# M of batch 1's third chunk, made after the states' reads instead of beside M of batch 0's last chunk

## The chip, the cores and the metric

The kernel runs on one core of one Trainium2 chip. The metric is the device time of one execution in microseconds (us), taken as the median of several runs. Four runs of the kernel before are given; they lie between 710.19 and 710.21 us, with a median of 710.2 us.

## What is computed

The reference is an attention block whose result is fed through a feed-forward block. Cut to what matters (B = 8 batches, H = 8 heads, S = 512 tokens, 32 states, D = 64 per head, so a row of 512 after the heads are joined, and d_ff = 2048):

```
a      = softmax(scale * x @ state.T)        # over the 32 states
xread  = a @ state                           # (B, H, 512, 64)
a2     = softmax(scale * state @ x.T)        # over the 512 tokens
sread  = a2 @ x                              # (B, H, 32, 64)
rows   = concatenate([xread, sread], axis=2) # heads joined: 4352 rows of 512
h      = rows @ w_in
g      = h * sigmoid(1.702 * h)
out    = g @ w_out
```

## The kernel before

**How the work is cut.** xread is never formed. Since xread @ w_in = a @ (state @ w_in), the kernel first makes, for a batch b and one of four chunks c of 512 columns of d_ff, the product M(b, c) of the states with that part of w_in (`att_M`, matmuls by `by_state`, line L320). Then `up_x` (through `up`, L524) multiplies M by the transposed softmax aT to get 128 rows of h for all 512 tokens, and ScalarE applies the activation (L527) into a buffer g. Four `up_x` steps use one chunk of M; sixteen make one batch's g. `down` (L542) multiplies g by w_out into four PSUM banks, one for each 128 tokens.

**What one M takes.** M(b, c) has two halves of 128 x 512 numbers, each filling one PSUM bank. Its sixteen matmuls use 64 rows and 32 columns of TensorE's array each. They are issued in two passes of eight, which run side by side. ScalarE then copies the two banks to the SBUF tile M (L460), and only after its copy is a bank free.

**Which banks.** Two banks are in the pool psA (tag `att`), and two in psH (tag `h`). `up_x` takes a bank of psH, or one of psA where it is called with `spare`. `att_M` takes both banks of psA, or both of psH with `spare` (its third argument True). The remaining four banks hold scores and then the results of `down`.

**Order.** Every engine works off its own list of instructions in the order in which the program writes them; the order is written out by hand. For batches 0 and 1 it is: a first part that loads, rounds the weights and makes scores; then `turn(b, c, then, n, more)`, which does the four `up_x` of chunk c of batch b and, ahead of the last of them, makes the M named in `then` (and in `more`); `rounds` brings in pieces of w_out, seven VectorE instructions for each (L207 to L243). The call that matters is the one for batch 0, chunk 2: ahead of its last `up_x` (h tile 11) it makes M(0, 3) in psA and M(1, 2) in psH.

After it, ScalarE does the four exponentials of the states' softmax (`att_s_exp`, L372), with a load of its table before and after; VectorE scales the results (`att_s_norm`, L378 to L381) and rounds more of w_out; TensorE does h tiles 12 to 15, which use M(0, 3). Then a loop over f (0 to 15) does the sixteen `down` steps of batch 0. Between them, at f = 0, stand four groups of transposes (`att_eT`, L489); at f = 1 the states' reads of batches 0 and 1 (`att_sread`, matmuls L500 into one bank of psA each, ScalarE's copy L506) and then M(1, 3) in psA; at f = 2 two small transposes (`att_srT`, L514) and the first `up_x` that reads M(1, 2), h tile 8 of batch 1; the other `up_x` of batch 1 follow at f = 3, 5, 7 and so on.

From batch 1's own `down` on, a fixed sequence of Strassen products follows (`strassen_two`, `strassen_low`, `up_strassen`; L738, L689, L1051), with the next batch's attention hung in at named points ("P2a", "P5.1", "run").

Of the kernel before, what the change touches and what calls it, by code (L numbers as in the profile page):

```python
# [20 lines left out]
def kernel(  # L21
# [70 lines left out]
    def att_ps(shape, name):  # L92
        return psA.tile(shape, FP32, tag="att", name=name)
# [36 lines left out]
    def load_state(b):  # L130
        stn[b] = apool.tile([P, NG, D], FP32, tag="stn", name=f"stn_{b}", bufs=2)
        for g in range(NG):
            nc.sync.dma_start(stn[b][:, g], st_v[b, g])
# [9 lines left out]
    def load_x_squares(b):  # L143
        xsq[b] = xpool.tile([P, NPR, S], FP32, tag="xn", name=f"xsq_{b}")
        for g in range(NG):
            for k in range(D // Ns):
                o = D * g + Ns * k
                dst = xsq[b][o : o + Ns].rearrange("p j (t a) -> p j t a", a=Ns)
                for j in range(NPR):
                    nc.sync.dma_start(dst[:, j], x_sq[b, g, k][:, j])  # L150

    def turn_x(b):

        A[b]["xT"] = xsq[b]
        for j in range(NPR):
            nc.vector.transpose(xsq[b][:, j], xsq[b][:, j])
# [106 lines left out]
    def round_to(n, ahead=AHEAD):  # L263

        nin = NFC * NPR
        while done["b"] < min(n, len(PIECES)):
            i = done["b"]
            powers_to(i + 1)
            round_b(i, min(i + 1 + ahead, max(nin, i + 1)), i + 1 < nin and (i + 1 < n or i >= NPR))
            done["b"] += 1  # L270
            while done["b"] > NPR and done["load"] < len(PIECES) and before(done["load"]) < done["b"]:
                load_weights(done["load"] + 1)
# [42 lines left out]
    def by_state(b, ps, rhs):  # L315

        for j in range(NPR):
            for g in range(NG):
                rows, st = slice(D * g, D * (g + 1)), slice(Ns * j, Ns * (j + 1))
                nc.tensor.matmul(ps[g][st], A[b]["stT"][rows, st], rhs(rows, j), start=True, stop=True)  # L320
# [32 lines left out]
    def att_s_max(b):  # L353
        a = A[b]
        a["mx2"] = []
        for g in range(NG):
            mx = apool.tile([P, 1], FP32, tag="mx2", name=f"mx2_{b}_{g}", bufs=4)
            nc.vector.tensor_reduce(out=mx, in_=a["s"][g], axis=AX.X, op=ALU.max, negate=True)
            nc.vector.tensor_scalar(mx, mx, scale, None, ALU.mult)
            a["mx2"].append(mx)  # L360
# [90 lines left out]
    def att_M(b, c, spare=False):  # L451

        m = mpool.tile([P, NG, FC], FP32, tag=f"M{turns['M'] % NFC if b < 2 else c}", name=f"M_{b}_{c}")
        turns["M"] += 1
        A[b]["M", c] = m
        name = f"M_{b}_{c}_"
        ps = [psH.tile([P, FC], FP32, tag="h", name=name + str(g)) if spare else att_ps([P, FC], name + str(g)) for g in range(NG)]
        by_state(b, ps, lambda rows, j: w_in[c][rows, j])
        for g in range(NG):
            nc.scalar.copy(m[:, g], ps[g])  # L460
# [21 lines left out]
    def att_eT(b, g):  # L482

        a = A[b]
        if g == 0:
            a["eT"] = apool.tile([P, NG, SCH, P], FP32, tag="e1" if b else "eT", name=f"eT_{b}")
        ps = att_ps([P, SCH, P], f"eT_{b}_{g}")
        for c in range(SCH):
            nc.tensor.transpose(ps[:, c], a["e2"][g][0][:, P * c : P * (c + 1)], ident)  # L489
        nc.scalar.copy(a["eT"][:, g], ps)  # L490

    def att_sread(b):

        a = A[b]
        ps = att_ps([P, NG, D], f"sr_{b}")
        for g in range(NG):
            for c in range(SCH):
                for j in range(NPR):
                    st = slice(Ns * j, Ns * (j + 1))
                    nc.tensor.matmul(  # L500
                        ps[st, g], a["eT"][:, g, c, st], xn[b][:, c, NG * j + g],
                        start=(c == 0), stop=(c == SCH - 1),
                    )
        sr = apool.tile([P, P], FP32, tag="sr", name=f"sr_{b}", bufs=2)
        if b < 2:
            nc.scalar.copy(sr, ps.rearrange("p g d -> p (g d)"))  # L506
        else:
            for g in range(NG):
                nc.scalar.activation(out=sr[:, D * g : D * (g + 1)], in_=ps[:, g], func=AF.Copy, scale=a["e2"][g][1])
        A[b]["sr"] = sr  # L510

    def att_srT(b):
        ps = att_ps([P, P], f"srT_{b}")
        nc.tensor.transpose(ps, A[b]["sr"], ident)  # L514
        nc.scalar.copy(srT[:, :, b, :], ps.rearrange("p (j n) -> p j n", j=NPR))
# [13 lines left out]
    def up_x(b, f, spare=False):  # L529
        c, o = divmod(P * f, FC)  # L530
        m = A[b]["M", c]
        up(b, f, S, [m[:, g, o : o + P] for g in range(NG)], [A[b]["aT"][:, g] for g in range(NG)], spare)
# [3 lines left out]
    def down(key, r, fs, dst, last):  # L536

        if fs[0] == 0:
            O[key, r] = bank_o[r]
        ops = O[key, r]  # L540
        for f in fs:
            nc.tensor.matmul(  # L542
                ops, G[key, f // 2][:, f % 2, P * r : P * (r + 1)], w_out[:, f], start=(f == 0), stop=(f == NF - 1)
            )
            if last and f < HF and f % 2:
                free.append(G.pop((key, f // 2)))
        if fs[-1] == NF - 1:
            osb = opool.tile([P, DM], FP32, tag="osb", name=f"osb_{key}_{r}")
            nc.scalar.copy(osb, ops)
            nc.sync.dma_start(dst, osb)  # L550
# [9 lines left out]
    def s12(key, u, ntok):  # L560

        half = ntok // 2
        (a11, a21), (_, a22) = quarters(key, u, ntok), quarters(key, HF // 2 + u, ntok)
        s1, s2 = S1[:, 2 * u : 2 * u + 2, :half], S2[:, 2 * u : 2 * u + 2, :half]
        nc.vector.tensor_tensor(out=s1, in0=a21, in1=a22, op=ALU.add)
        nc.vector.tensor_tensor(out=s2, in0=s1, in1=a11, op=ALU.subtract)
# [109 lines left out]
    def low_third(t):  # L676
        _, b12, _, b22 = halves_of(t)
        T_of(b12, b22, b12)
# [441 lines left out]
    def rounds(n):  # L1120
        round_to(done["b"] + n)
# [44 lines left out]
    round_to(NPR + 1)  # L1166
    att_x_norm(1)

    def turn(b, c, then, n=(), more=None):

        for i in range(nper):
            if i == nper - 1 and then:
                att_M(*then)
                if more:
                    att_M(*more)
            up_x(b, nper * c + i)
            if i < len(n):
                rounds(n[i])
# [6 lines left out]
    round_to(4 * NPR)  # L1185
    att_s_max(0)
    att_s_max(1)
    turn(0, 2, (0, 3), more=(1, 2, True))
    room = apool.tile([P, NPR, S], FP32, tag="xT", name="e2_01")
    att_s_exp(0, room[:, :NG])  # L1190
    att_s_exp(1, room[:, NG:])
# [12 lines left out]
    def T_of(t, x0, x1):  # L1204
        nc.vector.tensor_tensor(out=t, in0=x0, in1=x1, op=ALU.subtract)

    def low_made(k, t, i):

        for fn, args in low_sums(t, (low_a, low_b)[i]):
            fn(*args)  # L1210
        low_keep(k, turn_rooms[i])

    def low_away(k, t):

        room = apool.tile([P, NPR, S], FP32, tag="xT", name=f"away_{k}").rearrange("p j t -> p (j t)")[:, : 3 * FC]
        for fn, args in low_sums(t, low_parts(room)):
            fn(*args)
        low_keep(k, room)
# [3 lines left out]
    for f in range(NF):  # L1222
        rounds(1)
        round_to(NFC * NPR + f + 1)
        if f == NF - 1:

            up_x(1, rest.pop(0))
        for r in range(SCH):
            down(0, r, [f], out_x[0, r], r == SCH - 1)
        if f == 0:  # L1230
            for b in range(2):
                for g in range(NG):
                    att_eT(b, g)
        if f == 1:

            att_sread(0)
            att_sread(1)
            att_M(1, 3)
        if f == 2:
            att_srT(0)  # L1240
            att_srT(1)
        if f == 2 or f % 2 == 1 and 1 < f < NF - 1:
            up_x(1, rest.pop(0))
        if f == HF:
            load_state(2)
            load_x_squares(2)
        if f == NF - 2:
            T_of(T1, B12, B11)
            low_away(6, B22)
            low_made(5, T1, 1)  # L1250
            for u in range(NU - 1):
                s12(1, u, S)
            T_of(T2, B22, T1)
            low_third(T1)
            for u in range(NU - 1):
                s3(1, u, S)
            T_of(B12, B22, B12)
            low_away(3, T3)
            low_third(T3)
        if f == NF - 1:  # L1260
            turn_x(2)
            low_made(2, T2, 0)
# [73 lines left out]
```

## Time and profile before

| | |
|---|---|
| median of the runs | 710.2 us |
| the profiled execution's own time | 710.21 us |
| its span, first to last instruction | 708.4 us |
| TensorE (PE) busy | 695.9 us, 98% of the span |
| VectorE (DVE) busy | 601.9 us, 85% |
| ScalarE (ACT) busy | 231.3 us, 33% |
| DMA traffic | 77.89 MB, mean 110 GB/s |

The profiled execution took 1.8 us more than its span, which lies ahead of the first and after the last instruction. PE stands for matmuls, PEld for the loads of their weights (the stationary operand), which overlap matmuls. A tile's number is left out in the rows: all M tiles, PSUM banks of M included, are called M. An "idle before" names what ended the wait. Busy time of a pipelined matmul overlaps that of its neighbour, so for TensorE the distance from one start to the next is what counts.

### The profile page before, as it was taken

Reading aid. Unit: us, or ns where it says so; the run is one execution under the profiler, and the core shown is the slowest. Engines: PE = TensorE matmul, PEld = TensorE weight load, DVE = VectorE, ACT = ScalarE, POOL = GpSimd, SP = SyncE. Lnnn points to the kernel's source line nnn. Section 1 sums busy time; section 2 is a strip of 40 time slices with the busy share of each in tenths; the row PEclk is TensorE's granted clock in tenths of the full one; section 3 lists DMA queues with packets and bytes.
Section 4 is the critical chain, followed back from the end, with each engine's and each line's share of the span. In section 5 each row is a group of like instructions: output and inputs, shape, how many; then the busy total and the mean of one; then the engine's idle time right before and its main releaser. Section 6 shows DMA issues by size and latency. Waiting matters only on the chain.

```text
span 708.4 us, 12667 instructions
## 1 busy us (share of the span) xinstructions
PE 695.9 (98%) x4973; PEld 558.0 (79%) x4975; DVE 601.9 (85%) x1246; ACT 231.3 (33%) x456; POOL 0.8 (0%) x8
## 2 busy tenths in 40 slices
PE   8989999999999999999999999999999999999996
PEld 3433444458998799879998899889987998899995
DVE  6999699999978998799978996899789987888650
ACT  5686610014224412423233423341243224300210
POOL 0000000000000000000000000000000000000000
PEclk9999999999999999999999999999999999999999
DMA  9921246318742384409550664148432840041001
GB/s 234 366 71 57 82 149 146 126 75 206 217 118 44 61 194 136 79 1 206 153 107 1 142 189 119 20 80 197 137 53 45 193 152 16 0 121 60 16 1 29
DMA packets 143914, 77.89 MB, mean 110 GB/s; under 512 B 113904, under 2 KB 127728, under 8 KB 143856
## 3 DMA queue, kind: packets, MB, share of 16 engines
q1 hardware_dynamic: 143856, 77.09, 41.6%
q8 instruction: 39, 0.64, 0.4%
q14 instruction: 19, 0.16, 0.1%
HBM read 61.08 MB, written 15.99 MB: 109 GB/s over the span
## 4 chain that ended last, share of the span: by engine, by line
PE 96%; ACT 2%; DMA 1%; DVE 0%; issue 0%; DVEq 0%
PE low L689 21%; PE o L1051 17%; PE o L738 14%; PE o L689 10%; PE o L542 8%; PE h L524 7%; PE upx L1051 6%; PE M L320 4%; PE o L585 2%; PE warm L125 2%; PE o L320 1%; PE sr L500 1%; PE upx_sr L1051 1%; DMA out_dram<-osb_sr 1%; ACT M L460 1%; ACT low L219 1%
## 5 line engine op out<-in xcount | busy, mean ns | idle before, releaser
L1061 DVE TENSOR_TENSOR g<-o,g 128x512 f32<-128x512 f32 (+1 forms) x140 | 88.0, 650 | 51.1 <-PE o L1051 50.2
L738 PE MATMUL o<-w_out,g 128*128 128x256 f32 x448 | 100.5, 380 | 0.0
L738 PEld LDWEIGHTS o<-w_out,g 128*128 128x128 f32 x448 | 84.2, 190 | 16.9 <-issue 5.5
L1058 ACT ACTIVATE g<-g 128x512 f32<-128x512 f32 (+1 forms) x84 | 49.8, 600 | 100.8 <-DVE g L1061 100.8
L1051 PE MATMUL upx<-aT,M 128*128 128x256 f32 x192 | 49.3, 379 | 0.0
L1051 PE MATMUL o<-ta,M 128*128 128x256 f32 x192 | 49.3, 379 | 0.0
L1051 PE MATMUL o<-ta,ms 128*128 128x256 f32 x192 | 48.3, 379 | 0.0
L689 PE MATMUL low<-low,g 128*128 128x128 f32 x336 | 44.4, 275 | 0.0
L689 PEld LDWEIGHTS low<-low,g 128*128 128x128 f32 x336 | 40.9, 192 | 0.0
L460 ACT COPY M<-M 128x512 f32<-128x512 f32 x64 | 33.1, 597 | 23.3 <-PE M L320 23.3
L1051 PEld LDWEIGHTS o<-ta,ms 128*128 128x128 f32 x192 | 36.5, 190 | 5.0
L1051 PEld LDWEIGHTS o<-ta,M 128*128 128x128 f32 x192 | 36.5, 190 | 5.0
L1051 PEld LDWEIGHTS upx<-aT,M 128*128 128x128 f32 x192 | 36.0, 190 | 4.6
L689 PE MATMUL low<-sums,later 128*128 128x128 f32 x280 | 37.0, 275 | 0.0
L689 PEld LDWEIGHTS low<-sums,later 128*128 128x128 f32 x280 | 34.6, 192 | 0.4
L320 PE MATMUL M<-w_in,stT 64*32 64x512 f32 x512 | 32.4, 594 | 0.0
L527 ACT ACTIVATE g<-h 128x512 f32<-128x512 f32 x24 | 14.0, 592 | 54.7 <-PE h L524 54.7
L524 PE MATMUL h<-low,M 128*128 128x512 f32 x64 | 29.5, 597 | 1.5 <-DVE low L408 1.5
L524 PE MATMUL h<-aT,M 128*128 128x512 f32 x64 | 28.7, 599 | 2.3 <-ACT M L460 2.3
L689 PE MATMUL low<-w_out,g 128*128 128x128 f32 x224 | 29.6, 275 | 0.0
L542 PE MATMUL o<-w_out,g 128*128 128x512 f32 x64 | 28.6, 594 | 0.0
L542 PE MATMUL o<-w_out,sums 128*128 128x512 f32 x64 | 28.3, 592 | 0.0
(210 smaller groups left out, 1295.7 us busy)
## 6 DMA issues: line engine op xcount, KB each, us to landing
low<-low SPq DMA_DIRECT2D x78, 256.0 KB, 3.5
later<-in_moe_w_out_dram SPq DMA_DIRECT2D x16, 512.0 KB, 3.3
xn<-in_x_dram SPq DMA_DIRECT2D x28, 256.0 KB, 4.8
low<-low SPq DMA_DIRECT2D x9, 768.0 KB, 4.0
w_out<-in_moe_w_in_dram SPq DMA_DIRECT2D x12, 512.0 KB
xsq<-in_x_dram SPq DMA_DIRECT2D x96, 64.0 KB, 2.3
out_dram<-osb SPq DMA_DIRECT2D x18, 256.0 KB, 2.8
out_dram<-later SPq DMA_DIRECT2D x14, 256.0 KB, 2.2
```

Of the source, the lines that this page charges most:

```text
L125: nc.tensor.matmul(ps, zeros[:, :P], zeros, start=True, stop=True)
L320: nc.tensor.matmul(ps[g][st], A[b]["stT"][rows, st], rhs(rows, j), start=True, stop=True)
L460: nc.scalar.copy(m[:, g], ps[g])
L524: nc.tensor.matmul(hps, lhs[i], rhs[i], start=(i == 0), stop=(i == n - 1))
L527: nc.scalar.activation(out=G[key, f // 2][:, f % 2, :ntok], in_=hps, func=AF.Gelu_apprx_sigmoid)
L542: nc.tensor.matmul(ops, G[key, f // 2][:, f % 2, P * r : P * (r + 1)], w_out[:, f], start=(f == 0), stop=(f == NF - 1))
L585: nc.tensor.matmul(ps[:, r], lhs[f][:, P * r : P * (r + 1)], rhs[:, f], start=(first and r == 0 and f == 0), stop=(f == HF - 1), skip_grou ...
L689: nc.tensor.matmul(ps, lhs[f], rhs[:, f], start=(first and f == 0), stop=(f == QF - 1), skip_group_check=True)
L738: nc.tensor.matmul(ps[:, r], lhs[f][:, P * r : P * (r + 1)], rhs[:, f], start=(r == 0 and f == 0), stop=(f == HF - 1), skip_group_check=True,)
L1051: nc.tensor.matmul(ps[:, k], lhs[i][:, o : o + P], rhs[i], start=(first and k == 0 and i == 0), stop=(i == n - 1), skip_group_check=True,)
L1058: nc.scalar.activation(out=dst, in_=src, func=AF.Gelu_apprx_sigmoid)
L1061: nc.vector.tensor_tensor(out=dst, in0=ps, in1=x, op=ALU.add)
```

## The change

M(1, 2) is no longer made in the turn of batch 0's third chunk. It is made at f = 1 of the loop over `down`, after the two states' reads and ahead of M(1, 3). It still takes the two banks of psH, and M(1, 3) those of psA. The SBUF tile that it is copied to is given out in turn by a counter; since M(1, 2) still comes after M(0, 3) and ahead of M(1, 3), each M gets the same tile as before. The parameter `more` of `turn` goes.

```diff
-    def turn(b, c, then, n=(), more=None):
+    def turn(b, c, then, n=()):
 
         for i in range(nper):
             if i == nper - 1 and then:
                 att_M(*then)
-                if more:
-                    att_M(*more)
             up_x(b, nper * c + i)
             if i < len(n):
                 rounds(n[i])
...
     att_s_max(0)
     att_s_max(1)
-    turn(0, 2, (0, 3), more=(1, 2, True))
+    turn(0, 2, (0, 3))
     room = apool.tile([P, NPR, S], FP32, tag="xT", name="e2_01")
...
             att_sread(0)
             att_sread(1)
+            att_M(1, 2, True)
             att_M(1, 3)
         if f == 2:
```

Moved are, on TensorE, 16 weight loads and 16 matmuls of L320, and on ScalarE two copies of L460. VectorE, GpSimd and the DMA queue of SyncE keep their instructions and their order.

## The prediction

> **What bounds the kernel now.** I read the page's chain of work first: it says who ended last.
>
> ```profile
> PE 96%; ACT 2%; DMA 1%; DVE 0%; issue 0%; DVEq 0%
> ```
>
> TensorE is the bound almost everywhere, so a microsecond that TensorE does not wait, or does not work, counts in full unless something else then comes late. Next I read the places where the chain is not TensorE's. This is the same chain around the change (start, length, engine and line), in order of time:
>
> ```profile
> 68.25 1.16 PE M L320 x16
> 69.40 1.55 ACT M L460 x3
> 70.95 0.04 issue
> 71.00 8.85 PE h L524 x20
> ```
>
> The reader is to see that the chain leaves TensorE for 1.55 us and comes back: three copies of M by ScalarE. The timeline of TensorE shows the place (start, busy, then what was waited for), and further down where M(1, 3) stands:
>
> ```profile
> 68.17 1.95 PE L320 MATMUL M<-w_in,stT 64*32 64x512 f32 x32
> 71.00 8.85 PE L524 MATMUL h<-aT,M 128*128 128x512 f32 x20 [0.87 <-ACT M L460]
> ...
> 88.90 1.10 PE L500 MATMUL sr<-xn,eT 128*32 128x64 f32 x64
> 89.82 1.08 PE L500 MATMUL sr<-sums,eT 128*32 128x64 f32 x64
> 90.83 1.54 PE L320 MATMUL M<-w_in,stT 64*32 64x512 f32 x16
> 92.30 3.70 PE L542 MATMUL o<-w_out,g 128*128 128x512 f32 x8
> ```
>
> At 68.17 stand M(0, 3) and M(1, 2), 32 matmuls. The next up step, h tile 11, needs a bank of psH, and M(1, 2) has just filled both. So it waits 0.87 us until ScalarE has copied M(0, 3)'s two banks and the first of M(1, 2)'s. A lone M of 16 should not take 1.54 us either; the waits of the weight loads tell why (total, times, longest):
>
> ```profile
> PEld M L320 <- ACT sr L506: 0.3, 1, 0.3
> ```
>
> M(1, 3) takes the psA banks of the states' reads just before it, and its second matmul (start 91.28, the first at 90.83) waits for the copy of the second read, which ends at 91.23.
>
> Last, the other engines after 70 us. VectorE's waits from 60 to 300 us hold one long one:
>
> ```profile
> DVE sm L378 <- ACT e L372: 5.7, 1, 5.7
> ```
>
> It ends at 75.74. From there VectorE has no idle row until 201.73, where it waits for a product of TensorE. That is a resource that could turn into the bound, so its start matters.
>
> **What the Trainium skill says.** "PSUM — Partial Sum Buffer", The four PSUM rules: one matmul output fits in one bank of 512 fp32 values. The trace agrees: M's halves are 128x512 f32, so an M needs both banks of its pool. "TensorE: Matmul & The Clock Gate", Part 3, The mechanism: matmuls keep strict order. The trace agrees: behind tile 11 nothing else of TensorE ran in the 0.87 us. "TensorEngine Tiling (Array Packing)", Key Properties: a change of tiling mode drains the array. Seen here: from M's second pass to the following 128*128 matmul it is 0.57 us, against 0.43 us between equal ones. The change keeps the number of such switches, so they cost nothing new. "ScalarE: Activation LUTs", What ACT_TABLE_LOAD costs: neighbouring ACTIVATEs overlap by about 93 ns. The trace agrees for the copies here: about 0.59 us each, started 0.48 us apart.
>
> **The change part by part.** All sums are of the profiled execution, 710.21 us with its span of 708.4; the median of the runs is 710.2, so both give the same forecast.
>
> Taken away at 68.17. M's passes start at 68.175, 68.628, 69.058 and 69.487, so M(1, 2) holds TensorE for two passes of 0.43, 0.86 us. Tile 11 starts at 70.996. A lone M between up steps is in the trace twice: the one at 60.092 has its up step at 61.111, the one at 51.883 at 52.903, each 1.02 us later. So tile 11 starts at 68.175 + 1.02 = 69.19, earlier by **1.80 us**: 0.86 of work and 0.94 of waiting (from start to start; the row's 0.87 counts from the modelled end).
>
> What might be late next there? Tile 11 then takes the bank of tile 9, whose activation ended at 67.17. Tile 12 needs M(0, 3): its copies start at 69.38 whether or not M(1, 2) follows and end at 70.45; tile 12 comes at 69.19 + 0.53 + 3 x 0.43 = 71.01. Tile 13 takes tile 11's bank at about 72.7; the activation of tile 11 comes 1.80 earlier, at 71.22 to 71.82, because the ScalarE copies ahead of it end at 70.45. Tiles 14 and 15 take psA, free from 70.45. No new wait, with 0.3 us the tightest margin.
>
> ScalarE's run follows tile 11: activation at 73.02, table load 73.63, four exponentials to 77.73, table load, four activations to 81.09. It all moves by 1.80, and VectorE's start at 75.74 with it, to 73.94. No weight load is waited for there: the DMA of a w_out piece lands in 3.3 us and is issued four pieces (four times 3.5 us of VectorE) ahead.
>
> Added at 90.83. M(1, 2) starts straight after the reads into psH, idle since about 80. M(1, 3) follows two passes later, 0.88 us after 90.83, when the reads' copies (ended at 91.23) are done: it no longer waits. The price of such a pair is in the trace: in the run of batch 2 the same sequence (read, M in psH, M in psA) takes 191.33 to 193.21, 1.88 us; the pair at 165.87 takes 1.85. Against that stand the present 90.83 to 92.30, 1.47 us. So this place gets **0.40 us** longer (0.38 by the other pair): 0.86 of work less 0.45 of wait that it covers.
>
> Copies of L460: two leave the window at 70.3 to 71.4 and two go ahead of M(1, 3)'s, in a stretch where ScalarE is idle from 91.23 to 92.45 and from 93.52 to 96.15. In the new times M(1, 2)'s copies end at about 91.3 and M(1, 3)'s at 92.4, while the two small transposes that want psA come at 95.84 - 1.40 = 94.4 and tile 8, which wants M(1, 2), at 94.7. They cost nothing: the eight down matmuls of f = 1 (3.5 us) cover them; without that cover the price would be the two copies, 1.1 us.
>
> From then on TensorE runs 1.40 us early and VectorE 1.80, so what TensorE takes from VectorE comes no later relative to it. What ScalarE and the DMAs do for batch 0's outputs and the next attention starts from TensorE or VectorE and moves with them. TensorE has no wait in the trace from 85 us to the end, so there is nothing further to gain there.
>
> Sum: - 1.80 + 0.40 = **- 1.40 us** (- 1.42 with the other pair). 710.2 - 1.4 = **708.8 us**, a span near 707.0. A measurement of this kernel can tell about 0.2%, 1.42 us, from no change: the forecast lies on that line.
>
> What the trace before does not show is M in psH straight after reads in psA at this very place. Lower bound: hidden, so that only the 1.80 counts, 708.4; but two passes of a busy array can't vanish, and I leave it little. Upper bound: M(1, 2) adds 0.86 and M(1, 3) still waits, 709.3. I take 0.40 because batch 2's sequence is the same code.
>
> **The rivals.**
>
> 1. *The added M is paid in full.* If M(1, 3) still meets its wait of 0.45, the net is - 1.80 + 0.86 = - 0.94: 709.3 us. For it: that wait is on record. Against: it ended at 91.23, ahead of 90.83 + 0.88 = 91.71.
>
> 2. *The gain is given back to VectorE's chain.* At 171.28 the first low product of batch 1 ends in a ScalarE copy (172.38 to 172.65) behind exponentials that end at 172.22 and hang on VectorE's maxima (170.46); the product at 173.07 needs that copy. If VectorE did not move, TensorE could gain there only 0.16 (copy behind the exponentials) + 0.38 (copy's end to its use) = 0.54 us: 709.7. For it: VectorE is unbroken up to there. Against: that unbroken run begins with what tile 11 releases, so it moves by 1.80.
>
> 3. *Slower: tile 8 waits for its M.* TensorE is in order, and behind tile 8 of batch 1 stand all the down steps of batch 0. It decides from the point at which M(1, 2)'s second copy ends later than 94.7; to come out slower by 0.2% it must end 1.40 + 1.42 = 2.8 us after that, at 97.5, for 711.6 us. For it: the M is now made 22 us later than before, close ahead of its first reader. Against: a margin of 3.4 us, and ScalarE has only two reads' copies of 0.27 us there.
>
> 4. *It does not free tile 11.* If something else ended as late, the time would stay near 710.2. Against: the bank of tile 9 and M(0, 2) are both long ready.
>
> **How the numbers follow.** Main case, 708.6 to 709.0: 0.79. As its sum is 1.40 to 1.42 and the line is 1.42, I split it, 0.47 beyond and 0.32 within, the larger part to small things that also move up (pieces of waits under 0.1 us that no row names). A larger gain, down to 708.4: 0.04. Rival 1: 0.07; rival 2: 0.05; rival 4: 0.02; rival 3: 0.03. Faster by over 0.2%: 0.47 + 0.04 = 0.51. Within: 0.32 + 0.07 + 0.05 + 0.02 = 0.46. Slower: 0.03. The range takes the main case, the larger gain and rival 1: 708.4 to 709.3.
>
> **What would show it.** In the profile after: one M of 16 matmuls before tile 11, with no wait on ACT M L460, tile 11 at 69.2; the long VectorE wait cut from 5.7 to 3.9 us; at about 89.0 a row of 32 M matmuls, 1.88 us to the next down matmul, with no wait on ACT sr; TensorE's down at f = 2 and the start of the Strassen products 1.40 us early, and the end too. A wait of tile 8 or of the small transposes on ACT, a wait of TensorE on VectorE after 150 us, or an M at 89 that takes over 2.2 us would make it wrong.

## The result and the profile after

The changed kernel takes 708.87 us (median of 31 runs, 708.58 to 709.34) beside 710.23 us for the kernel before, run along with it: 1.36 us less, a ratio of 0.9981 with an interval of 0.9976 to 0.9986. Run again beside later experiments it took 708.88 against 710.21 us, a ratio of 0.9981 (0.9974 to 0.9989). The forecast was 708.8 us.

The profiled execution has a span of 706.9 us. TensorE's timeline around tile 11, and around M(1, 2)'s new place:

```profile
68.10 1.09 PE L320 MATMUL M<-w_in,stT 64*32 64x512 f32 x16
69.12 2.84 PE L524 MATMUL h<-aT,M 128*128 128x512 f32 x6
...
87.95 1.08 PE L500 MATMUL sr<-sums,eT 128*32 128x64 f32 x64
88.95 1.95 PE L320 MATMUL M<-w_in,stT 64*32 64x512 f32 x32
90.83 3.70 PE L542 MATMUL o<-w_out,g 128*128 128x512 f32 x8
94.37 0.38 PE L514 MATMUL srT<-ident,sr 128*128 128x128 f32 x2
94.59 1.88 PE L524 MATMUL h<-low,M 128*128 128x512 f32 x4
```

One M of 16 matmuls stands ahead of tile 11, and the row of tile 11 has no wait any more. From M's start to tile 11 it is 69.12 - 68.10 = 1.02 us. At 88.95 stand the 32 matmuls of M(1, 2) and M(1, 3); the down step follows 1.88 us later. The chain that ended last no longer leaves TensorE here:

```profile
68.17 1.02 PE M L320 x16
69.19 8.78 PE h L524 x20
...
89.02 1.88 PE M L320 x32
90.90 3.63 PE o L542 x8
```

ScalarE's timeline shows the copies of both M's in a row, done at 92.18, ahead of the small transposes at 94.37 and of tile 8 at 94.59:

```profile
90.13 2.05 ACT L460 COPY M<-M 128x512 f32<-128x512 f32 x4 [0.78 <-PE M L320]
94.68 0.43 ACT L515 COPY srT<-srT 128x128 f32<-128x128 f32 x2 [2.49 <-PE srT L514]
```

And VectorE's long wait (total, times, longest) is shorter by 1.9 us:

```profile
DVE sm L378 <- ACT e L372: 3.8, 1, 3.8
```

The two traces can be laid side by side, instruction by instruction. TensorE of the changed kernel is 0.07 us early from the arrival of the first data on. It is 1.88 us early at tile 11 (- 1.80), 1.47 at the down step after the two M's (+ 0.41), and 1.52 from the sixth low product of batch 1 on (- 0.05). The low products are groups of eight matmuls (L689, `strassen_low`), each 0.89 us after the one before. So the trace shows 1.45 us from the first data on, and the medians 1.36. The arrival of the first data alone differs between the kept traces, from 0.10 us earlier to 0.18 us later than in the kernel before, so what counts below is how far an offset moves, not its size; the tenth of a us between the trace and the medians is not explained.

### The profile page after: what moved, and what is told of

Its sections match the earlier page's. It is cut to its first block, busy times and chain, and to the rows that moved or that the text cites. A ratio compares the mean times of both kernels' runs of the same rounds, so it can differ in the third digit from the quotient of the medians.

```text
span 706.9 us, 12667 instructions
## 1 busy us (share of the span) xinstructions
PE 694.7 (98%) x4973; PEld 557.4 (79%) x4975; DVE 602.3 (85%) x1246; ACT 231.0 (33%) x456; POOL 0.8 (0%) x8
## 4 chain that ended last, share of the span: by engine, by line
PE 95%; ACT 2%; DMA 2%; SPq 0%; DVE 0%; issue 0%; DVEq 0%
PE low L689 21%; PE o L1051 17%; PE o L738 14%; PE o L689 10%; PE o L542 8%; PE h L524 7%; PE upx L1051 6%; PE M L320 4%; PE o L585 2%; PE o L320 1%; PE sr L500 1%; PE warm L125 1%; PE upx_sr L1051 1%; DMA out_dram<-osb_sr 1%; DMA xn<-in_x_dram 1%; ACT low L219 1%
## 5 line engine op out<-in xcount | busy, mean ns | idle before, releaser
L689 PE MATMUL low<-low,g 128*128 128x128 f32 x336 | 44.4, 275 | 0.0
L689 PEld LDWEIGHTS low<-low,g 128*128 128x128 f32 x336 | 40.9, 192 | 0.0
L460 ACT COPY M<-M 128x512 f32<-128x512 f32 x64 | 33.1, 597 | 23.1 <-PE M L320 23.1
L689 PE MATMUL low<-sums,later 128*128 128x128 f32 x280 | 37.0, 275 | 0.0
L689 PEld LDWEIGHTS low<-sums,later 128*128 128x128 f32 x280 | 34.6, 192 | 0.4
L320 PE MATMUL M<-w_in,stT 64*32 64x512 f32 x512 | 32.0, 594 | 0.0
L689 PE MATMUL low<-w_out,g 128*128 128x128 f32 x224 | 29.6, 275 | 0.0
```

The costliest lines, as they stand in the source:

```text
L689: nc.tensor.matmul(ps, lhs[f], rhs[:, f], start=(first and f == 0), stop=(f == QF - 1), skip_group_check=True)
```

## The experiments

The medians below stand beside those of the kernel before, run along with them: 710.39 us for the first four, 710.33 for the next three, 710.21 for the last two.

### The wait alone

```diff
-            up_x(b, nper * c + i)
+            up_x(b, nper * c + i, bool(more) and i == nper - 1)
```

> The kernel before, with M(1, 2) left in the turn beside M(0, 3), but tile 11 of batch 0 put in a bank of psA, which M(0, 3)'s first copy frees at 69.97. Theory (the gain at tile 11 is 0.94 us of wait and 0.86 us of moved matmuls): only the wait goes, TensorE goes from the second M to tile 11 in 0.57 us, tile 11 starts 0.94 us earlier, at about 70.05, and nothing changes at f = 1 (M(1, 3) still 1.47 us to the next down matmul): 709.3 us. Rival (the wait is not the bank's but M's data or ScalarE's turn): tile 11 still starts near 71.0 and the time stays at 710.2 us.

Measured: 709.41 us, a ratio of 0.9986 (0.998 to 0.9993), 0.98 us less. TensorE's timeline of this kernel:

```profile
68.21 1.95 PE L320 MATMUL M<-w_in,stT 64*32 64x512 f32 x32
70.09 1.98 PE L524 MATMUL h<-aT,M 128*128 128x512 f32 x4
...
89.92 1.54 PE L320 MATMUL M<-w_in,stT 64*32 64x512 f32 x16
91.39 0.70 PE L542 MATMUL o<-w_out,g 128*128 128x512 f32 x1
```

The edit gives tile 11 a bank of psA and changes nothing else. With both M's still ahead of it, tile 11 starts 1.88 us after the first M's start, without a wait; in the kernel before that distance was 70.996 - 68.175 = 2.82 us. The difference is the 0.94 of the sum. The f = 1 place still takes 1.47 us. So the wait was for a bank, it is worth 0.94 us by itself, and it makes two thirds of the change's gain.

### M(1, 2) after M(1, 3)

```diff
-            att_M(1, 2, True)
             att_M(1, 3)
+            att_M(1, 2, True)
```

> The changed kernel, with M(1, 2) made after M(1, 3) instead of ahead of it at f = 1. Theory (M(1, 2) covers M(1, 3)'s wait of 0.45 us for the copy of the second states' read): the wait is back, the pair takes 0.45 us longer, some 2.33 us from the reads to the next down matmul instead of 1.88, and the time is 0.45 us over the changed kernel's: 709.3 us. Rival (the order of the two does not matter, since a pair takes 1.88 us anyhow): 708.9 us.

Measured: 709.35 us, 0.9985 (0.9979 to 0.9992), 1.04 us less than before. TensorE's timeline:

```profile
89.11 2.40 PE L320 MATMUL M<-w_in,stT 64*32 64x512 f32 x32
91.44 0.70 PE L542 MATMUL o<-w_out,g 128*128 128x512 f32 x1
```

The pair takes 91.44 - 89.11 = 2.33 us, 0.45 more than with M(1, 2) first; the medians of this kernel and the changed one, 0.48 apart, are not from runs taken together. The M that needs no bank of the reads has to stand ahead of the one that does. This is rival 1's price, and its cause.

### M(1, 2) next to its reader

```diff
-            att_M(1, 2, True)
             att_M(1, 3)
         if f == 2:
             att_srT(0)
             att_srT(1)
+            att_M(1, 2, True)
```

> The changed kernel, with M(1, 2) made at f = 2 right ahead of its first reader, tile 8 of batch 1, and M(1, 3) alone at f = 1. Theory (rival 3 of the prediction: TensorE stands still in front of tile 8 until ScalarE has copied M, where nothing lies between): from M's first matmul 1.8 to 2.3 us to tile 8 instead of 1.0, and M(1, 3)'s wait of 0.45 us is back; - 1.80 + 1.8 to 2.3 + about 0.1 for one more switch of tiling: 710.3 to 710.8 us, no gain left. Rival (a copy right behind its M is hidden by the weight load and the switch): 709.4 us.

Measured: 710.43 us, 1.0001 (0.9993 to 1.0009): no gain. TensorE's timeline:

```profile
94.53 1.09 PE L320 MATMUL M<-w_in,stT 64*32 64x512 f32 x16
96.34 1.98 PE L524 MATMUL h<-low,M 128*128 128x512 f32 x4 [0.73 <-ACT M L460]
```

From M to tile 8 it is 1.81 us, where an M without such a wait has 1.02; the row shows 0.73 of it as a wait on ScalarE. Rival 3's mechanism is real; what keeps the changed kernel from it is the eight down matmuls, 3.54 us, between M and its reader.

### VectorE held where it was

```diff
+    held = srT.rearrange("p j b n -> p (j b n)")[:, :S]
+    nc.vector.memset(held, 0.0)
     att_s_norm(0)
     att_s_norm(1)
+    for _ in range(3):
+        nc.vector.tensor_tensor(out=held, in0=held, in1=held, op=ALU.add)
```

> The changed kernel, with three additions of 128 x 512 put into VectorE's list after the scaling of the states' softmax, on rows of a tile that are overwritten later; about 1.8 us of extra work in VectorE's unbroken run, so that it stands again where it stood in the kernel before, while TensorE is early. Theory of the prediction (TensorE has 0.54 us to spare to VectorE's chain at the first low product of batch 1): TensorE is held there until it has lost about 0.86 us of its 1.40: 709.7 us. Rival (the spare time is larger than the chain read from the trace says): no TensorE wait there, 708.9 us.

Measured: 710.95 us, 1.0008 (1.0 to 1.0016). Both expectations missed: the whole gain is gone and a little more. The clearing of the rows (`memset`) falls into VectorE's wait and moves nothing. The additions moved VectorE 2.05 us, which puts it 0.16 to 0.21 us later than in the kernel before. TensorE's timeline at the low products of batch 1 has two waits:

```profile
172.63 1.16 PE L689 MATMUL low<-sums,later 128*128 128x128 f32 x8 [0.89 <-ACT pu L698]
...
175.91 1.16 PE L689 MATMUL o<-sums,spare_M 128*128 128x128 f32 x8 [0.28 <-DVE spare_M L694]
```

The first is the one that the prediction priced, and it cost about what it said: TensorE was 0.02 us early against the changed kernel and is 1.04 to 1.20 us late there, against 0.86 and the extra 0.2 us of VectorE. The second was not in the prediction. It comes three products later and takes TensorE to 1.74 us late. Against the kernel before, TensorE is then 0.22 us late, as much as VectorE. The median stands 0.56 us over the kernel before. Of that some 0.3 us lie outside the span: the runs of this kernel take 2.1 us more than their spans, those of every other kernel here 1.8. What takes that time no trace shows, and it is not part of the reading. ScalarE's timeline shows how the first arises, the copy `pu` going straight behind exponentials that waited for VectorE's maxima:

```profile
170.86 0.69 ACT L372 ACTIVATE e<-o,mx 128x512 f32<-128x512 f32 x1 [1.47 <-DVE mx L359]
...
172.23 0.19 ACT L372 ACTIVATION_READ_ACCUMULATOR e<-o,mx 128x1 f32 x1
172.32 0.26 ACT L698 COPY pu<-low 128x128 f32<-128x128 f32 x1
```

### One addition in the kernel before, and one in the changed kernel

The theory was formed anew: the sixth low product of batch 1 needs `spare_M`, the result of an addition (L694) in VectorE's list, and in the kernel before there was no time to spare at all. Its lines on VectorE and on TensorE are these:

```profile
175.36 0.28 DVE L694 TENSOR_TENSOR spare_M<-o,pu 128x128 f32<-128x128 f32 x1
175.75 1.11 PE L689 MATMUL o<-sums,spare_M 128*128 128x128 f32 x8
```

Both kernels have the edit above with `range(1)`.

> The kernel before with one addition of 128 x 512 (about 0.68 us) put into VectorE's list after the scaling of the states' softmax, on rows of a tile that are overwritten later. New theory (in the kernel before, TensorE already hangs by VectorE at the sixth low product of batch 1, which waits for an addition that ends 0.1 us ahead of it, so there is no time to spare): the whole 0.68 us is lost there, 0.68 us over the kernel before in this comparison, with a wait of TensorE on VectorE near 176. Theory of the prediction (0.54 us to spare): about 0.14 us are lost.

> The changed kernel with the same one addition. New theory (the changed kernel has only the 0.40 to 0.45 us by which VectorE moved further than TensorE): about 0.25 us are lost at the sixth low product, the time is 0.25 us over the changed kernel's, and VectorE's additions at that place stand 0.1 us ahead of their products. Theory of the prediction (0.54 and 0.40 us to spare): nothing is lost.

Measured: the kernel before with one addition takes 710.90 us, 1.0008 (1.0 to 1.0016), 0.57 us more. Against the kernel before, both engines start 0.10 us late. At the addition VectorE is 0.73 us late, so it moved by 0.63. TensorE is 0.24 us late after the third and fourth products, and 0.73 us from the sixth on, so it lost 0.63, all that VectorE moved. The 0.14 at the third and fourth is what the prediction's theory gave; the rest it did not have. VectorE's timeline and TensorE's, of this kernel:

```profile
175.48 0.69 DVE L745 TENSOR_TENSOR later<-later 128x512 f32<-128x512 f32 x1
176.09 0.28 DVE L694 TENSOR_TENSOR spare_M<-o,pu 128x128 f32<-128x128 f32 x1
```

```profile
176.43 1.16 PE L689 MATMUL o<-sums,spare_M 128*128 128x128 f32 x8 [0.28 <-DVE spare_M L694]
```

The addition ends at 176.37 and the product starts at 176.43. In the kernel before, the addition ended at 175.64 and the product started at 175.75: no wait row is shown, but from its second matmul on the product was already some 0.05 us late. So the kernel before had nothing to spare to VectorE, and the new theory holds.

The changed kernel with one addition takes 709.10 us, 0.9983 (0.9977 to 0.999). Against the changed kernel, its trace has TensorE go from 0.11 to 0.39 us late at the sixth product. VectorE moved by 0.65 us and TensorE lost 0.28, so some 0.37 were to spare; the new theory had a loss of 0.25. The changed kernel's own lines say the same:

```profile
173.59 0.29 DVE L694 TENSOR_TENSOR spare_M<-o,pu 128x128 f32<-128x128 f32 x1
174.28 1.06 PE L689 MATMUL o<-sums,spare_M 128*128 128x128 f32 x8
```

The addition ends at 173.88 and the product starts 0.40 us later. The two medians, 709.10 and 708.87, are not from runs taken together, and their difference is smaller than their intervals; the trace carries this reading.

### The transposes in two pools

```diff
-        ps = att_ps([P, SCH, P], f"eT_{b}_{g}")
+        ps = psH.tile([P, SCH, P], FP32, tag="h", name=f"eT_{b}_{g}") if b else att_ps([P, SCH, P], f"eT_{b}_{g}")
```

> The changed kernel with batch 1's two groups of transposes at f = 0 put in psH instead of psA, so that the third group does not wait for ScalarE's copy of the first. Theory: the wait of 0.24 us in front of the third group goes, TensorE is 0.24 us earlier from there on and VectorE is not, which leaves VectorE 0.2 us ahead at the low products: 0.24 us under the changed kernel. Rival (the copies of the second read come late next, or VectorE is met first): no difference to the changed kernel.

Measured: 708.50 us, 0.9975 (0.9966 to 0.9984), 1.83 us under the kernel before. The interval overlaps the changed kernel's, so that it is faster than that one rests on the trace. The changed kernel's transposes stand in two rows of TensorE's timeline, with a wait:

```profile
81.24 1.04 PE L489 MATMUL eT<-ident,e 128*128 128x128 f32 x8
82.52 1.14 PE L489 MATMUL eT<-ident,e 128*128 128x128 f32 x8 [0.24 <-ACT eT L490]
83.50 3.60 PE L542 MATMUL o<-w_out,g 128*128 128x512 f32 x8
```

This kernel's stand in one row, without a wait:

```profile
81.39 1.91 PE L489 MATMUL eT<-ident,e 128*128 128x128 f32 x16
83.14 3.60 PE L542 MATMUL o<-w_out,g 128*128 128x512 f32 x8
```

From the first transpose to the next down matmul it is 1.75 us; in the changed kernel 83.50 - 81.24 = 2.26. So 0.51 us were won, twice the 0.24 of the wait's row; against the changed kernel's trace TensorE goes from 0.15 us late to 0.36 us early. But at the sixth product TensorE goes from 0.36 us early to 0.17 us early: 0.19 us are given back to VectorE, whose addition ends at 173.95 with the product at 174.01. About 0.3 us are left.

### The VectorE steps of P5 later

```diff
-            for fn in first[i - 1 : i]:
+            for fn in first[i - 3 : i - 2] if i > 2 else ():
```

The last kernel has this beside the transposes' edit, and the changed kernel ran with it once more.

> The kernel with batch 1's transposes in psH, and in every Strassen pass the five VectorE steps of the list `first` in P5 (s4 and third_of) start after the third low product instead of after the first, so that two fewer of them, some 1.3 us, stand ahead of the addition that the sixth low product needs. Theory (TensorE is met by VectorE only there): the 0.19 us that the transposes' kernel lost at the sixth low product comes back, 0.5 us under the changed kernel, and no wait on VectorE in P5. Rival (the steps are then late for P6, or another addition takes their place): not under the changed kernel by more than 0.3 us, with a new wait of TensorE later in P5 or P6.

> The changed kernel once more, on the same chip as the next run, as a measure for it: 1.4 us under the kernel before.

Measured: the changed kernel took the 708.88 us given above, 1.33 us under the kernel before. The other took 715.18 us, 1.007 (1.0057 to 1.0084), far worse. The sixth product did come free: against the transposes' kernel TensorE goes there from 0.15 to 0.34 us early, which is the returned 0.19. But the steps that were put off now stand ahead of a later addition, and TensorE stands still for it in each of six batches (total, times, longest):

```profile
PE low L689 <- DVE later L694: 4.1, 6, 0.7
```

In batch 1 this puts TensorE from 0.11 us early to 0.73 us late, and each later batch adds about 1.1 us. The rival was right. The addition is the one that the thirteenth low product needs, and the earlier traces had shown its place: it ended 0.11 us ahead of that product in the kernel before (181.95 and 182.06), in the changed kernel (180.43 and 180.53) and in the transposes' kernel (180.26 and 180.37), so there too next to nothing was to spare. Of the kernels run, the one with the transposes in two pools has the lowest median.

## Why the prediction was right, point by point

**Tile 11, - 1.80 us.** Measured - 1.80. Its parts were 0.94 of wait and 0.86 of moved work; the run with the wait alone gave 0.94 for the first.

**f = 1, + 0.40 us.** Measured + 0.41. That M(1, 2) covers a wait of 0.45 was tested by turning the two M's around, which brought it back.

**Copies at no cost.** They end at 92.18, 2.2 us ahead of the small transposes. The prediction had 92.4 and 94.4.

**VectorE moves along.** Its long wait fell from 5.7 to 3.8 us; 3.9 was forecast. This proved to be a condition of the gain and not a by-product: with VectorE held back, TensorE's lead was gone by the sixth low product.

**Rival 2's price was wrong.** The prediction said that with VectorE unmoved TensorE could still gain 0.54 us, so 709.7. The step that failed is the margin: it was read at the third low product alone. The sixth product waits for an addition in VectorE's own list, and there the margin was zero, so the honest price of that rival was the whole 1.40, some 710.2. The held kernel showed it: with VectorE 0.21 us later than in the kernel before, TensorE came 0.22 us later too (its median, 710.95, has the 0.3 us outside the span as well). At the third product itself the 0.54 held. Its part of 0.38 is less than the distance of the two times named for it, 173.07 - 172.65 = 0.42, but in the held kernel too the product starts 0.05 us after the end of that copy (172.58 and 172.63). The wrong margin did not hurt the forecast because VectorE moved by more than TensorE.

**"Nothing further to gain" was not quite right.** The prediction said that TensorE had no wait from 85 us on. At the sixth product about 0.05 us lay below what the wait rows name, and came on top of the 1.40. The wait of the transposes, just ahead of 85 us, is in none of its terms; it is worth 0.51 us from start to start, not the 0.24 of its row, and 0.3 of that is left after VectorE is met.

**One sign was named wrongly.** It said that no wait on ACT sr would be left at f = 1. The changed kernel still has that row, 0.3 us of a weight load for M(1, 3); but the matmul behind it was not late, since M(1, 2) kept the array busy.

**Why on the edge.** The sum of 1.40 us stood 0.02 us short of the line of 0.2%, and the result, 1.36 us or 0.19%, lies within. The prediction had leaned the other way, with 0.51 for a gain beyond the line, because small waits would move up too. They did, by 0.05 us in the trace, but that is less than the difference between trace and medians: the sum could not tell the side.

## What to carry to other kernels

A product that fills both banks of a pool shortly ahead of a step that needs one of them can put the copies on the path of an engine that keeps its order, as here at tile 11. Ask first for a place where the pool has been idle, where another instruction's wait can be covered by it, and where enough work lies between it and its first reader to hide its copies; then look at what the freed engine releases: here the gain held only because VectorE, which TensorE meets next, started earlier too. A margin between two engines is the smallest over all places where they meet, and one that is read at a single place, even the most visible, is an upper bound.

## What the runs showed of the hardware

At both places where a run took a wait of TensorE away, the idle time shown in the row was less than the wait cost from start to start: 0.87 us in the row and 0.94 in starts at tile 11, and 0.24 against 0.51 at the transposes, where the groups run as one stream once the wait is gone. And an addition can hold a product with no wait row at all: the sixth product lost 0.28 us in the changed kernel with one addition, and its row names no wait.
